# Attention and expert layers on one core: GpSimd's SBUF operations wait for VectorE's, in a new order

## The chip, the cores and the metric

The kernel runs on one core of one Trainium2 chip. The time is device microseconds of one execution; a figure for a kernel is the median of its runs. A core has five engines, each with its own queue of instructions: TensorE (PE, with its weight loads as PEld), VectorE (DVE), ScalarE (ACT), GpSimd (POOL) and SyncE (SP, which issues DMAs). GpSimd and VectorE both read and write SBUF; only VectorE of the two reads PSUM.

## The reference

Eight batches of eight heads, 576 positions, head size 64. Attention keeps only scores that lie within tau of the row's maximum; the rest go to -1e9 before the softmax. Its output, 4608 tokens of 512 values, goes through a layer of eight experts: tokens with a positive skip score go to the expert of the largest gate logit, the others pass through.

```python
scores = scale * np.matmul(q, k.transpose(0, 1, 3, 2))
thresh = np.max(scores, axis=-1, keepdims=True) - tau
scores = np.where(scores >= thresh, scores, -1000000000.0)
attn = np.exp(scores - np.max(scores, axis=-1, keepdims=True))
attn = attn / (np.sum(attn, axis=-1, keepdims=True) + 1e-09)
out = np.matmul(attn, v)
...
h = np.maximum(xc[mask] @ w1[e], 0.0)
y[mask] = gate_w[mask, None] * (h @ w2[e])
out[do_compute] = xc + y
```

## The kernel before

Work is laid out in 32 pairs of heads (`NG`, four pairs to a batch), each of nine steps. fp32 operands are split into a high and a low part, so that PE multiplies in faster types and adds the products.

For a pair, `plan_pair` (L455) loads q and k (raw), casts the high half (hl, L432 on VectorE or L430 on ScalarE) and subtracts for the low half (L487, GpSimd or VectorE, 576 columns each), and `plan_dist` and `plan_blk` let SP copy the parts to where PE reads them (QK, BD). `plan_score` (L675 to L725) computes scores once to find each row's maximum (mx, VectorE, L707), `plan_thresh` makes thresholds of them in small VectorE operations (L753 to L777), and `plan_weights` computes the scores again, transposed, with the threshold taken off (sps, L675), takes the exponential on ScalarE (e, L840), masks it on VectorE (p, L845), casts two blocks of it to fp16 (phh, 1152 columns, L430 on ScalarE or L432 on VectorE) and subtracts for the low part on GpSimd (phl, L882; tph and tpl are the same for the tail rows, 576 columns). `plan_av` multiplies with V (L909, L912, L913; L913 is the one that reads phl), and GpSimd scales the result by the reciprocal sums (xb at L958, x at L971). `plan_v` loads V of a batch (vraw), finds its largest value on VectorE (L590) and splits it (Vl, L652, GpSimd). Once per two batches, and twice at the end, `plan_gate` works out each token's expert and list slot in some twenty small VectorE operations (L1140 to L1236), and GpSimd scatters records with indirect DMAs (lst, L1264). `plan_early` (L1343 on) picks one expert early, gathers tokens for it and splits its first weights in eight pieces (L1412); `plan_sort` orders the others.

Score banks in PSUM are two of `sps` and two of `shp`: PE's next score waits until VectorE has read one. `p` has two buffers, freed by GpSimd's phl; phh and phl have three, freed by PE.

All of these steps, up to some 700 us, are first handed to a planner (`Plan`) as operations with a cost on each engine that may run them, and dependencies. `place` then goes through time: for each engine it looks at operations that could start, and puts the one with the best rank in the next slot. `port` marks an operation that uses the SBUF port which VectorE and GpSimd share: every GpSimd operation by default except indirect DMAs (`port=()`), and the VectorE operations marked `BOTH` (casts and subtractions with both operands in SBUF, gate operations). `held` keeps, for each of the two engines, when its last such operation ends, and the other engine's next such operation isn't placed before that. So in the plan these operations of the two engines never overlap. The rank comes from keys (`OFF` shifts them), and then from `SEEDS`: each seed shifts ranks of the order reached so far, by small random amounts, and plans again. The order of the last pass is the one in which the instructions are written to the engines' queues; between engines only the dependencies through data become semaphore waits.

Behind the planned stage, from some 700 us on, the other experts run in a hand-written order that doesn't pass through `Plan`.

Of the kernel before, what the change touches and what calls it, by code (L numbers as in the profile page):

```python
# [73 lines left out]
DISS = 0.65  # L74
ENGINES = ("PE", "DVE", "ACT", "POOL", "SP")
PEER = {"DVE": "POOL", "POOL": "DVE"}
SEEDS = (
    3000017, 3000028, 3000035, 3000067, 3001483, 3019621, 3115975, 3117104, 3144197,
)
DLAT = 0.9  # L80
OFF = dict(
# [3 lines left out]
class Op:  # L85
    def __init__(self, key, fn, eng, lat, off, port):
        self.key, self.fn, self.eng, self.lat, self.off, self.port = key, fn, eng, lat, off, port
        self.deps, self.succ = [], []
        self.t0 = self.t1 = self.on = self.rev = None
        self.xfer = ()  # L90

    def ready(self, e):
        r = 0.0
        for d, order in self.deps:
            x = d.t0 if order else d.t1 + d.latency(e)
            r = x if x > r else r
        return r
# [21 lines left out]


class Plan:
    def __init__(self):
        self.ops, self.rings = [], {}

    def take(self, name, bufs):
        return [(name, bufs)]
# [26 lines left out]
        o.xfer = xfer  # L153
        return o

    def place(self, links, options, ready, rank, put):
        free = dict.fromkeys(ENGINES, 0.0)
        cand = {e: [] for e in ENGINES}
        held = dict.fromkeys(PEER, 0.0)
        wait = [len(a) for a, _ in links]  # L160

        def add(i):
            for e in options(i):
                cand[e].append((ready(i, e), rank(i, e), i))

        for i, n in enumerate(wait):
            if not n:
                add(i)
        for _ in links:
            best = None  # L170
            for e in ENGINES:
                c = cand[e]
                if not c:
                    continue
                h = held[PEER[e]] if e in PEER else 0.0
                if h > free[e]:
                    c = [(h, k, i) if r < h and e in self.ops[i].port else (r, k, i) for r, k, i in c]
                m = max(free[e], min(c)[0]) + LOOK
                x = min((x for x in c if x[0] <= m), key=lambda x: (x[1], x[0]))
                t = max(free[e], x[0])  # L180
                if best is None or t < best[0]:
                    best = (t, e, x[2])
            t, e, i = best
            free[e] = put(i, e, t, free[e])
            if e in PEER and e in self.ops[i].port:
                held[e] = free[e]
            for q in options(i):
                cand[q] = [x for x in cand[q] if x[2] != i]
            for q in links[i][1]:
                wait[q] -= 1  # L190
                if not wait[q]:
                    add(q)

    def forward(self, rank, emit=False):
        link = 0.0

        def put(i, e, t, _):
            nonlocal link
            o = self.ops[i]
            o.t0, o.on = t, e  # L200
            o.t1 = end = t + o.eng[e]
            for n, x in enumerate(o.xfer):
                link = max(link, t + (n + 1) * o.eng[e] / len(o.xfer) + DISS) + x
                o.t1 = link
            if emit:
                code = o.fn.__code__
                o.fn(e) if code.co_argcount and code.co_varnames[0] == "e" else o.fn()
            return end

        self.place(self.fore, lambda i: self.opts[i], lambda i, e: self.ops[i].ready(e), rank, put)  # L210
        return max(o.t1 for o in self.ops)

    def backward(self):
        link = 0.0

        def put(i, e, t, was):
            nonlocal link
            o = self.ops[i]
            if o.xfer:
                s = max(t, link)  # L220
                link = s + sum(o.xfer)
                o.rev = s + o.length()
                return max(was, t) + o.eng[e]
            o.rev = t + o.eng[e]
            return o.rev

        ops = self.ops
        self.place(
            self.back, lambda i: (ops[i].on,), lambda i, e: ops[i].latest(), lambda i, e: -ops[i].t1, put
        )  # L230
        return [-o.rev for o in ops]

# [30 lines left out]
def attn_moe_kernel(ctx: ExitStack, tc: tile.TileContext, qk, vl, tau, wg, w1, w2, out):  # L263
    nc = tc.nc
# [137 lines left out]
    NG = B * HP  # L402
    END = STEP * NG

    pl = Plan()
    PE, DVE, ACT, POOL, SPQ = "PE", "DVE", "ACT", "POOL", "SP"
    BOTH = (DVE, POOL)

    def wtile(dt, name):
        return wraw.tile([P, WW], dt, name=name, tag="wr")  # L410
# [17 lines left out]
    def copy(e, dst, src):  # L428
        if e == ACT:
            nc.scalar.activation(dst, src, AF.Copy)  # L430
        else:
            nc.vector.tensor_copy(dst, src)  # L432
# [865 lines left out]
    class Job:  # L1298
        def __init__(self, cap, rec, ids, idg):
            self.cap, self.rec, self.ids, self.idg = cap, rec, ids, idg  # L1300
            self.nb = -(-cap // P)
# [41 lines left out]
    def plan_early(k, j):  # L1343
# [22 lines left out]
        o = T["rec0"] = pl.dma(k, l0, T["scs0"] + [(T["pick"],)], [0.1])  # L1366
# [5 lines left out]
        o = pl.op(k + 1, ids, [o], {DVE: 0.15})  # L1372
# [12 lines left out]
        hs, ls = [], []  # L1385
# [12 lines left out]
        for n in range(8):  # L1398
            i, q = divmod(n, 4)
            d, fs = n // 2, slice(n % 2 * ns, n % 2 * ns + ns)  # L1400

            def hi(e, i=i, q=q, d=d, fs=fs):
                if i == 0 and q == 0:
                    early["wh"] = ep.tile([P, nv], F32R, name="wh0", tag="vraw")
                if d == 3 and fs.start == 0:
                    early["w3"] = ep.tile([P, 2 * S], F32R, name="w3", tag="raw")
                copy(e, w_h(d, fs), early["raw"][i][:, q * ns : q * ns + ns])

            def lo(e, i=i, q=q, d=d, fs=fs):
                if q == 0:  # L1410
                    wls[i] = wtile(F32R, "wl0")[:, 0 : 2 * F]
                (nc.gpsimd if e == POOL else nc.vector).tensor_tensor(  # L1412
                    w_l(d, fs), early["raw"][i][:, q * ns : q * ns + ns], w_h(d, fs).bitcast(F32), op=ALU.subtract
                )

            deps = ring.take("vraw", 1) if n == 0 else [(hs[0],)]
            if n == 6:
                deps = deps + ring.take("raw", 1)
            hs.append(pl.op(k + 4 + n, hi, [ld1 if i else T["pick"]] + deps, {ACT: 0.52, DVE: 0.33}, port=BOTH))
            deps = [(ls[-1],)] if q else ring.take("wr", WRB)  # L1420
            ls.append(pl.op(k + 5 + n, lo, hs[-1:] + deps, {POOL: 1.225, DVE: 0.6}, port=BOTH))
            if n == 3:
                ring.free("wr", hs[0:4] + ls[0:4])
# [229 lines left out]
    ms.enter_context(tc.manual_schedule(engines={ET.PE, ET.DVE, ET.Activation, ET.Pool, ET.SP}))  # L1653
    pl.run(SEEDS)

# [373 lines left out]
```

## Time and profile before

| | us |
|---|---|
| median of 3 runs | 992.52 (987.98 to 994.86) |
| the profiled execution | 992.55 |
| its span, first to last instruction | 990.8 |
| PE busy | 889.1 (90%) |
| VectorE busy | 746.2 (75%) |
| GpSimd busy | 678.0 (68%) |
| ScalarE busy | 600.9 (61%) |
| mean granted TensorE clock | 0.962 |

Shares are means over stages with different limits, so they are read by stretch. An instruction's duration in the trace includes the time in which it has started and waits for its port. "Idle before" is time in which the engine had no instruction, and the releaser is what ended it.

### The profile page before, as it was taken

What the parts mean: (1) busy time and instruction counts of PE and PEld (TensorE: products, weight loads), DVE (VectorE), ACT (ScalarE), POOL (GpSimd) and SP (SyncE); (2) the same over time, 40 slices, a digit from 0 to 9 for tenths busy, and PEclk for the clock granted to TensorE, in tenths of its full rate; (3) what the DMA queues carried; (4) which work ended last, traced back from release to release, by engine and by line L of the source; (5) the groups of instructions that cost most, each with busy time, mean ns of one, the idle gap of its engine ahead of it and who ended that gap; (6) DMA issues with size and microseconds to landing.
All of it is one profiled execution on the core that took longest, in us unless ns stands there. A gap on an engine that the chain in (4) does not pass through costs nothing. (4 is left out here: it accounts for less than half of the span.)

```text
span 990.8 us, 24765 instructions
## 1 busy us (share of the span) xinstructions
PE 889.1 (90%) x9618; PEld 820.4 (83%) x9618; DVE 746.2 (75%) x1692; ACT 600.9 (61%) x880; POOL 678.0 (68%) x444
## 2 busy tenths in 40 slices
PE   6889999989999799899889898978869999999994
PEld 5689898888888798899878788877858998999993
DVE  6788888888888798988888998897444454567770
ACT  1567867956686596698688478657423423553440
POOL 5578987976689687689888577877633454654551
PEclk9799999999999999999999899999898999999997
DMA  7986687776449657766955954712337555535530
GB/s 200 216 195 150 141 223 173 163 225 150 102 103 250 143 128 209 202 144 149 263 112 125 275 136 88 179 20 103 113 99 247 156 179 192 180 122 182 174 127 17
DMA packets 81791, 157.37 MB, mean 159 GB/s; under 512 B 28620, under 2 KB 28876, under 8 KB 81673
## 3 DMA queue, kind: packets, MB, share of 16 engines
q1 hardware_dynamic: 76984, 145.49, 56.0%
q0 software_dynamic: 4544, 10.28, 3.2%
q8 instruction: 77, 1.26, 0.5%
q14 instruction: 42, 0.34, 0.1%
q10 hardware_dynamic: 144, 0.00, 0.0%
HBM read 70.78 MB, written 24.78 MB: 96 GB/s over the span
## 5 line engine op out<-in xcount | busy, mean ns | idle before, releaser
L882 POOL TENSOR_TENSOR phl<-p,phh 128x1152 f16<-128x1152 f32 x128 | 306.3, 2396 | 105.7 <-ACT phh L430 63.9
L840 ACT ACTIVATE e<-sps,ntau 128x576 f32<-128x576 f32 x288 | 209.1, 737 | 103.0 <-PE sps L675 92.4
L707 DVE TENSOR_REDUCE mx<-shp 128x1 f32<-128x288 f32 x558 | 238.0, 449 | 44.3 <-PE shp L702 39.5
L845 DVE SCALAR_TENSOR_TENSOR p<-sps,e 128x576 f32<-128x576 f32 x288 | 215.5, 750 | 35.1 <-ACT e L840 20.2
L702 PE MATMUL shp<-QK 128*128 128x288 f32 x992 | 207.0, 319 | 22.5 <-DVE mx L707 20.5
L675 PE MATMUL sps<-QK 128*128 128x288 f32 x1024 | 194.3, 315 | 19.5 <-DVE p L845 13.8
L702 PEld LDWEIGHTS shp<-QK 128*128 128x128 f32 x992 | 152.4, 195 | 34.3 <-DVE mx L707 29.0
L675 PEld LDWEIGHTS sps<-QK 128*128 128x128 f32 x1024 | 149.6, 194 | 30.1 <-DVE p L845 14.1
L430 ACT ACTIVATE phh<-p 128x1152 f16<-128x1152 f32 x107 | 124.2, 1161 | 32.9 <-DVE p L845 20.5
L913 PE MATMUL avp<-Vh,phl 128*128 128x65 f16 x1280 | 134.6, 196 | 8.1 <-POOL phl L882 8.0
L909 PE MATMUL avp<-Vh,phh 128*128 128x65 f16 x1280 | 136.8, 198 | 0.3 <-ACT a L430 0.3
L912 PE MATMUL avp<-Vl,phh 128*128 128x64 f16 x1280 | 135.4, 196 | 0.0
L913 PEld LDWEIGHTS <-phl 128*128 128x128 f16 x1280 | 120.3, 99 | 8.9 <-POOL phl L882 8.9
L909 PEld LDWEIGHTS <-phh 128*128 128x128 f16 x1280 | 119.0, 100 | 8.7
L912 PEld LDWEIGHTS <-phh 128*128 128x128 f16 x1280 | 120.5, 101 | 0.6 <-issue 0.4
L1682 POOL TENSOR_TENSOR wl<-wr,wh 128x1024 fp32r<-128x1024 f32 x28 | 72.5, 2605 | 34.7 <-ACT wh L1681 29.4
L1719 PE MATMUL hps<-xh,wl 128*128 128x256 f32 (+4 forms) x256 | 76.7, 300 | 0.0
L1719 PE MATMUL hps<-xh,wh 128*128 128x256 f32 (+4 forms) x248 | 76.0, 306 | 0.1
L1719 PE MATMUL hps<-xl,wh 128*128 128x256 f32 (+4 forms) x248 | 74.7, 301 | 0.0
L487 POOL TENSOR_TENSOR hl<-raw,hl 128x576 fp32r<-128x576 f32 x41 | 58.7, 1445 | 21.6 <-DVE gps L757 19.1
L1731 POOL DMA_INDIRECT out<-o,ids x21 | 21.0, 1002 | 71.6 <-DVE o L1730 30.1
L1720 ACT ACTIVATE QK<-hps 128x256 fp32r<-128x256 f32 (+4 forms) x64 | 27.0, 422 | 68.2 <-PE hps L1719 66.2
(261 smaller groups left out, 1957.4 us busy)
## 6 DMA issues: line engine op xcount, KB each, us to landing
QK<-hl SPq DMA_DIRECT2D x192, 288.0 KB
wr<-in_w SPq DMA_DIRECT2D x31, 1024.0 KB
raw<-in_qk SPq DMA_DIRECT2D x32, 576.0 KB
vraw<-in_vl SPq DMA_DIRECT2D x32, 384.0 KB
xs<-xb SPq DMA_DIRECT2D x32, 256.0 KB
out<-xb SPq DMA_DIRECT2D x32, 256.0 KB
BD<-hl SPq DMA_DIRECT2D x64, 64.0 KB
xs<-x SPq DMA_DIRECT2D x8, 128.0 KB
```

The costliest lines, as they stand in the source:

```text
L430: nc.scalar.activation(dst, src, AF.Copy)
L675: nc.tensor.matmul(ps[:, j, 0:HS], w_, x_[:, js], start=(i == 0), stop=(i == len(mm) - 1))
L702: nc.tensor.matmul(ps[:, 0:HS], w_, x_[:, js], start=(q == 0), stop=(q == len(mm) - 1))
L707: nc.vector.tensor_reduce(T["mx", g][:, o, j : j + 1], T.pop(("S", g, i, j))[:, 0:HS], AX.X, ALU.max)
L840: nc.scalar.activation(e, T["W", g, i][:, :, 0:HS], AF.Exp, bias=ntau, scale=0.125)
L845: nc.vector.scalar_tensor_tensor(T[z][:, kt % 2].rearrange("p (a b) -> p a b", a=2), T.pop(("W", g, i))[:, :, 0:HS], 0.0, T.pop(("e", g, i ...
L882: nc.gpsimd.tensor_tensor(T["pl", g, i], T.pop(z)[:, 0:nk], T["ph", g, i], op=ALU.subtract)
L909: nc.tensor.matmul(pv[:, c, :], x, Vh[:, hd, kt, :], start=(j + q + c == 0), stop=False, skip_group_check=True)
L912: nc.tensor.matmul(pv[:, c, 0:D], x, Vl[:, hd, kt, :], start=False, stop=False, skip_group_check=True)
L913: nc.tensor.matmul(pv[:, c, :], y, Vh[:, hd, kt, :], start=False, stop=(c == NM), skip_group_check=True)
L1682: lo[q % 2].tensor_tensor(w[1][:, sl], rs, w[0][:, sl].bitcast(F32), op=ALU.subtract)
L1719: nc.tensor.matmul(hp_[:, 0:cap], w_, x, start=(i == 0), stop=(i == len(mm) - 1))
```

## The change

Every operation is now written by `emit`, which notes the instructions that it makes. After a VectorE operation with `port`, the name of its last instruction is kept. The first instruction of the next GpSimd operation with `port`, in the order of the plan, gets a dependency on that name, hence a semaphore wait, and the name is cleared. Nothing is added in the other direction. In the plan, GpSimd's operation may start 0.165 us after the end of VectorE's (`LAG`; `GAL` is the mirrored figure of the backward pass). `SEEDS` is a new list, of 126 numbers in place of 9. The cast of the seventh weight piece gets an order-only dependency on the sixth's that creates its tile.

```diff
+LAG = {"DVE": 0.0, "POOL": 0.165}
+GAL = {"DVE": 0.165, "POOL": 0.0}
 SEEDS = (
-    3000017, 3000028, 3000035, 3000067, 3001483, 3019621, 3115975, 3117104, 3144197,
+    14000043, 14000049, 14000050, 14000051, 14000054, 14000501, 14000633, 14000634, 14000684, 14000705, 14000776,
...
 class Plan:
-    def __init__(self):
-        self.ops, self.rings = [], {}
+    def __init__(self, tc):
+        self.ops, self.rings, self.tc = [], {}, tc
+        self.last = None
+
+    def emit(self, o):
+        e, code, seen = o.on, o.fn.__code__, []
+        nc = self.tc.nc
+
+        def note(*a):
+            seen.append(a[-1])
+
+        nc.push_inst_callback(note)
+        o.fn(e) if code.co_argcount and code.co_varnames[0] == "e" else o.fn()
+        nc.remove_inst_callback(note)
+        if not seen:
+            return
+        if e == "DVE" and e in o.port:
+            self.last = seen[-1].name
+        elif e == "POOL" and e in o.port and self.last:
+            self.tc.add_manual_dep(
+                seen[0],
+                self.last,
+                mybir.DependencyInfo(mybir.DependencyClass.Sync, mybir.DependencyReason.DATA),
+                reason="VectorE reads SBUF first",
+            )
+            self.last = None
...
-                h = held[PEER[e]] if e in PEER else 0.0
+                h = held[PEER[e]] + lag[e] if e in PEER else 0.0
...
             if emit:
-                code = o.fn.__code__
-                o.fn(e) if code.co_argcount and code.co_varnames[0] == "e" else o.fn()
+                self.emit(o)
...
             if n == 6:
                 deps = deps + ring.take("raw", 1)
+            if n == 7:
+                deps = deps + [(hs[6],)]
```

## Rows read from the trace of the kernel before

**Rows 1.** Busy time by stretch: the stretch and its length in us, then busy us of each engine (number of instructions), the granted clock, the DMA share and GB/s.
```profile
40.00:700.00 660.00, 595.73 (x7699) 551.58 (x7699) 566.35 (x1369) 480.55 (x684) 521.91 (x303) 0.97 0.66 162
700.00:760.00 60.00, 50.69 (x444) 46.75 (x443) 22.99 (x70) 18.69 (x34) 25.96 (x22) 0.91 0.34 111
760.00:991.00 231.00, 215.97 (x1360) 199.25 (x1358) 131.07 (x187) 92.79 (x153) 113.01 (x66) 0.98 0.46 153
```

**Rows 2.** The timeline of VectorE and GpSimd from 438 to 443 us: start, duration, engine, line, operation, and in brackets the idle time before it and what ended it.
```profile
438.56 0.75 DVE L432 CAST phh<-p 128x1152 f16<-128x1152 f32 x1
...
441.13 1.05 DVE L432 CAST tph<-p 128x576 f16<-128x576 f32 x1
442.10 0.75 DVE L487 TENSOR_TENSOR hl<-raw,hl 128x576 fp32r<-128x576 f32 x1
...
439.48 2.38 POOL L882 TENSOR_TENSOR phl<-p,phh 128x1152 f16<-128x1152 f32 x1 [0.94 <-DVE phh L432]
442.26 1.74 POOL L882 TENSOR_TENSOR tpl<-p,tph 128x576 f16<-128x576 f32 x1 [0.39 <-DVE tph L432]
```

**Rows 3.** Groups of instructions by line and shape: count, busy us in all, mean ns of one, and idle time before them with its releasers.
```profile
L487 DVE TENSOR_TENSOR hl<-raw,hl 128x576 fp32r<-128x576 f32 x23 | 26.4, 1161 | 1.4 <-ACT hl L430 1.4
L432 DVE CAST phh<-p 128x1152 f16<-128x1152 f32 x21 | 16.5, 787 | 0.0
L432 DVE CAST hl<-raw 128x1152 fp32r<-128x1152 f32 x9 | 10.8, 1196 | 0.3
...
L1154 DVE TENSOR_SCALAR gw<-lg 128x9 f32<-128x9 f32 x3 | 0.5, 164 | 0.0
...
L882 POOL TENSOR_TENSOR phl<-p,phh 128x1152 f16<-128x1152 f32 x128 | 306.3, 2396 | 105.7 <-ACT phh L430 63.9 <-DVE phh L432 6.9 <-DVE ca L1164 4.6
```

**Rows 4.** The timeline of VectorE: five single instructions.
```profile
240.19 2.29 DVE L1193 TENSOR_SCALAR rec<-tokp 128x9 f32<-128x9 f32 x1
...
517.41 3.05 DVE L432 CAST hl<-raw 128x1152 fp32r<-128x1152 f32 x1
...
640.42 2.60 DVE L1173 CAST rs<-rs 128x8 bf16<-128x8 f32 x1
...
652.93 3.04 DVE L1221 TENSOR_TENSOR ca<-ca 128x32 f32<-128x32 f32 x1
...
660.79 2.56 DVE L1236 SCALAR_TENSOR_TENSOR si<-si 128x4 int32<-128x4 int32 x1
```

**Rows 5.** The timeline of GpSimd at the same places; x2 merges two instructions with no pause between them.
```profile
240.08 2.38 POOL L882 TENSOR_TENSOR phl<-p,phh 128x1152 f16<-128x1152 f32 x1
...
515.10 4.74 POOL L882 TENSOR_TENSOR phl<-p,phh 128x1152 f16<-128x1152 f32 x2
...
640.61 2.37 POOL L882 TENSOR_TENSOR phl<-p,phh 128x1152 f16<-128x1152 f32 x1
...
653.61 1.30 POOL L882 TENSOR_TENSOR tpl<-p,tph 128x576 f16<-128x576 f32 x1
654.85 1.06 POOL L958 TENSOR_TENSOR xb<-a,z 128x512 f32<-128x512 f32 x1
...
660.93 2.39 POOL L882 TENSOR_TENSOR phl<-p,phh 128x1152 f16<-128x1152 f32 x1
```

**Rows 6.** The timeline of VectorE and of GpSimd at 693 us.
```profile
692.98 5.17 DVE L1412 TENSOR_TENSOR wl<-raw,wh 128x512 fp32r<-128x512 f32 x1
...
692.90 4.70 POOL L882 TENSOR_TENSOR phl<-p,phh 128x1152 f16<-128x1152 f32 x2
```

**Rows 7.** The timeline of PE: the first instruction after each of nine gaps, with the gap in brackets.
```profile
243.17 0.85 PE L702 MATMUL shp<-QK 128*128 128x288 f32 x2 [1.89 <-DVE mx L707]
...
262.48 0.80 PE L675 MATMUL sps<-QK 128*128 128x288 f32 x4 [2.14 <-DVE p L845]
...
415.22 0.90 PE L702 MATMUL shp<-QK 128*128 128x288 f32 x4 [1.92 <-DVE mx L707]
...
520.96 0.53 PE L702 MATMUL shp<-QK 128*128 128x288 f32 x2 [2.88 <-DVE mx L707]
...
560.79 0.17 PE L1205 MATMUL gps<-rs,tri 128*128 128x8 bf16 x1 [2.54 <-DVE rs L1173]
...
614.34 0.77 PE L675 MATMUL sps<-QK 128*128 128x288 f32 x4 [2.03 <-DVE p L845]
...
643.08 0.17 PE L1205 MATMUL gps<-rs,tri 128*128 128x8 bf16 x1 [1.75 <-DVE rs L1173]
...
656.62 0.54 PE L702 MATMUL shp<-QK 128*128 128x288 f32 x2 [2.02 <-DVE mx L707]
...
664.40 0.80 PE L675 MATMUL sps<-QK 128*128 128x288 f32 x4 [2.85 <-DVE p L845]
```

**Rows 8.** Busy time by stretch, columns as in rows 1: one of five stretches with a low granted clock (243.13 to 246.54, 263.61 to 267.02, 560.57 to 567.40, 615.19 to 618.60, 666.39 to 673.22), and the sum of the five.
```profile
560.57:567.40 6.83, 6.37 (x49) 5.97 (x49) 5.71 (x16) 1.79 (x2) 3.52 (x3) 0.50 0.80 207
...
sum 23.89, PE 23.38 PEld 22.07 DVE 16.13 ACT 8.20 POOL 14.28; mean PE 4.68 PEld 4.42 DVE 3.23 ACT 1.64 POOL 2.85
```

**Rows 9.** Waits by who waited for whom over the whole span: us in total, times, and the longest in us.
```profile
DVE vmx L590 <- DMA vraw<-in_vl: 11.7, 8, 2.1
DVE p L845 <- POOL phl L882: 10.8, 7, 5.0
...
PE avp L913 <- POOL phl L882: 8.0, 6, 4.8
```

**Rows 10.** The timeline of GpSimd at 327 us.
```profile
327.69 0.40 POOL L971 TENSOR_TENSOR x<-a,z 64x128 f32<-64x128 f32 x1 [4.26 <-DMA lst<-rec,si]
```

More of the change, by code (lines that the diff above doesn't have):

```diff
@@ L154, in dma, with place @@
         return o
-    def place(self, links, options, ready, rank, put):
+    def place(self, links, options, ready, rank, put, lag):
         free = dict.fromkeys(ENGINES, 0.0)
@@ L205, in put @@
             if emit:
-                code = o.fn.__code__
-                o.fn(e) if code.co_argcount and code.co_varnames[0] == "e" else o.fn()
+                self.emit(o)
             return end
-        self.place(self.fore, lambda i: self.opts[i], lambda i, e: self.ops[i].ready(e), rank, put)
+        self.place(self.fore, lambda i: self.opts[i], lambda i, e: self.ops[i].ready(e), rank, put, LAG)
         return max(o.t1 for o in self.ops)
@@ L228, in backward @@
         self.place(
-            self.back, lambda i: (ops[i].on,), lambda i, e: ops[i].latest(), lambda i, e: -ops[i].t1, put
+            self.back, lambda i: (ops[i].on,), lambda i, e: ops[i].latest(), lambda i, e: -ops[i].t1, put, GAL
         )
@@ L403, in attn_moe_kernel @@
     END = STEP * NG
-    pl = Plan()
+    pl = Plan(tc)
     PE, DVE, ACT, POOL, SPQ = "PE", "DVE", "ACT", "POOL", "SP"
```

11 rows, old and new, of the table SEEDS are left out of this document.

## The prediction

> **What bounds the kernel now.** I read the page's busy shares first, then busy time by stretch. From 40 to 700 us (attention) PE works 595.73 of 660 us, VectorE (DVE) 566.35, GpSimd (POOL) 521.91; from 760 on the two vector engines have ample room [rows 1]. So PE is the bound of the attention stage, with 64.3 us of idle time in it, and VectorE is close behind. The change touches only the planned stage, so a gain has to come out of those 64.3 us, or out of TensorE's clock there.
>
> Next I asked which groups on VectorE are longer than their work. An SBUF subtraction of 576 columns takes 0.75 us when nothing disturbs it, at 442.10 [rows 2], but the mean of 23 is 1161 ns; the casts hl<-raw average 1196 ns where the equally wide phh<-p average 787; the small gate operations need about 0.16 us [rows 3]. GpSimd's long instruction, phl<-p, takes 2.4 us [rows 3]. Then I looked for single VectorE instructions that were far too long. Nine of them end a PE gap; five are shown [rows 4]: a cast of 128x8 takes 2.60 us, a 128x32 subtraction 3.04. Each time a GpSimd SBUF instruction starts close to VectorE's, before it (240.08 against 240.19) or even after it (640.61 against 640.42, 660.93 against 660.79), and is served first [rows 5]; at 517.41 the cast ends only with the second of two phl, at 652.93 the subtraction only with an xb that follows a tpl. The clearest pair stands at 693: one subtraction is held for 5.17 us by two phl that follow each other without a pause [rows 6]. So a VectorE instruction that is waiting does not get in when GpSimd's current instruction ends, if GpSimd has another one ready: it loses each of those races. The plan gives the two engines the SBUF port in turn, but nothing on the chip keeps that turn.
>
> Behind VectorE's held instruction stand the row maxima (mx) and masks (p) that free the score banks, and PE stops for them. The nine gaps are 1.89, 2.14, 1.92, 2.88, 2.54, 2.03, 1.75, 2.02 and 2.85 us, **20.0 us** together [rows 7], almost a third of PE's idle time of the stage. After five of them the granted clock is 0.50, the 1.2 GHz level, for 3.41 or 6.83 us: 23.89 us in all, with PE busy for 23.38 of it [rows 8]. At the upper level that work takes half, so these stretches cost up to **11.7 us**.
>
> **The change part by part.**
>
> *The wait.* A GpSimd SBUF instruction now starts after the VectorE SBUF instruction planned ahead of it. All nine cases look like a turn that was planned for VectorE and lost: VectorE's queue held ready mx and p behind the instruction, and a plan that gave GpSimd the first turn would have put those ahead. One of nine I leave out as doubtful. Of a gap, part is won back today, since the other engines catch up during it; the stage is idle for 44.3 of 660 us outside the nine, 6.7%, so PE has something, but not much, to win back from. I count two thirds as real, for gap and clock alike: (20.0 + 11.7) x 8/9 x 2/3 = **18.8 us gained**. The bounds are 0 (all of it comes back as other idle time) and 31.7 us.
>
> *What the wait costs.* Where VectorE is first today, GpSimd's instruction is issued and held by the port: the tpl at 442.26 takes 1.74 us, against 1.30 for one with the port to itself, and ends at 444.00 [rows 2, 5]. With the wait it would start 0.08 to 0.17 us after VectorE's end (those are the lags from tph, 441.13 + 1.05, to the tpl and from phh, 438.56 + 0.75, to the phl [rows 2]): 442.85 + 0.08 to 0.17 + 1.30 is 444.23 to 444.32, so 0.2 to 0.3 us more. I take at most 100 handovers (53 VectorE instructions of rows 3 and some ten in each of five runs of gate operations; the latter count is an estimate): 100 x 0.3 = 30 us of GpSimd's time at most, little over nothing at the least, where GpSimd is not ready yet anyway. GpSimd is idle for 138 us of the stage [rows 1], which covers it. Behind a waiting phl stand the next phl, the head's output scaling (xb, x) and the indirect DMAs of GpSimd's queue; PE's last matmuls of a head (L913) and, through the two p buffers, VectorE's own masks wait for phl. These waits are 8.0 us of PE's and 10.8 of VectorE's today [rows 9]. If GpSimd's lateness grows by 15 us, the middle of the bounds, and a fifth reaches PE: **3 us lost**, between 0 and 15.
>
> *The lag in the planner's costs* (0.165 us) adds no work; it is inside that price. *The order-only dependency of the seventh weight cast on the sixth* costs nothing: the two pieces come from one load, and their casts follow each other anyway; without that cover it is the wait for one cast of 512 columns, less than the 787 ns of a phh, which is over twice as wide [rows 3].
>
> *The new order.* All five queues are ordered afresh, SP's loads and GpSimd's indirect DMAs with them, while the count of instructions and bytes stays. I cannot see the new order in this trace. What it can shift is bounded by gaps unconnected with the port: VectorE waits 11.7 us for V loads, and the phl waits just named [rows 9]; together some 20 us with PE's share below that. I take no change, and 10 us either way for the range.
>
> The sum: -18.8 + 3 = -15.8. The profiled execution took 992.55 us (span 990.8 and 1.7 around it), and the median of the three runs is 992.52, so the same base serves. **Forecast 977 us.** The stage behind it is a chain of PE work that starts when attention ends, so the gain is carried to the end whole.
>
> **The port's rule.** By the Trainium skill (SBUF — State Buffer, section Who interferes with whom) the pair is locked for a whole instruction, and issue order decides who is blocked. By that, the VectorE instruction at 693 would have got in after the first phl, at 2.3 us; the trace has it in after the second, and so disagrees [rows 6].
>
> **The rivals.**
>
> *Served in order of arrival.* If the port does serve by arrival, and the four cases with GpSimd's last instruction starting after VectorE's own (517.41, 640.42, 652.93, 660.79) had another cause, their gaps of 2.88 + 1.75 + 2.02 + 2.85 = 9.5 us stay. By the same fractions the gain is then 10.5/20.0 of 18.8 = 9.9 less 3: 985.6 us. This is what the skill's rule above would make of it. Rows 6 speak against it. Chance 0.08.
>
> *The new order brings its own gaps.* The new order may meet V loads and phl at worse moments. With the 10 us of the bound lost, 977 becomes 987 to 990. For it: PE has 44 us of such gaps already. Against: nothing in the trace says that the present order is lucky. Chance 0.20.
>
> *Slower: GpSimd becomes the late one.* The wait hangs GpSimd on VectorE's queue, which itself waits for PE and ScalarE. The trace shows the price of a late GpSimd once: it stood for 4.26 us [rows 10], and the longest waits of rows 9 lie behind that, VectorE's mask with 5.0 us and PE with 4.8. If a VectorE instruction runs behind its planned time by one phl (2.4 us) at ten of the handovers and all of that reaches PE, 24 us are lost, with some clock (3.41 us at half, three times, 5 us): 977 + 29 = 1006 us. It decides once more than about six such waits reach PE whole. Against: 138 us idle on GpSimd, and three phh/phl buffers. Chance 0.14.
>
> *The change does nothing that PE sees,* because the held instructions were planned after GpSimd's: then the wait isn't on those pairs, and the time is 992 give or take the order. Against: the starts so close to each other, and the ready work behind. Chance 0.06.
>
> **How the numbers follow.** The forecast case has 0.52, with 966 to 984 as its own range. About 1%, 982.6 to 1002.4, is what a measurement of this kernel can tell from no change. Faster: nearly all of the forecast case (0.48), some of the order's case and of the arrival case (0.07), 0.55. Slower: the late GpSimd, 0.14. The rest, 0.31, is within 1%. The range starts at 962, the forecast with nearly the whole bound won, and goes up to 1000, past the order's own gaps; the slower rival stays outside.
>
> **What would show it.** The 2 to 5 us VectorE instructions on tiny gate operands are gone from the attention stage, and the mean of the subtraction (1161 ns) falls to below 0.9 us; rows of GpSimd carry idle time ended by VectorE's casts, subtractions and gate operations; PE's idle time from 40 to 700 falls from 64 to some 50 us and the clock's mean rises. The forecast is wrong if the held instructions vanish and PE's idle time stays: then waits for phl, or for loads, have grown by as much. It is also wrong if they remain.

## The result: 965 us, and the profile after

The changed kernel takes 965.21 us (median of 4 runs, 956.40 to 969.93) against 993.69 for the kernel before, measured beside it (median of 4, 987.98 to 996.08): ratio 0.9711 [0.9626, 0.9797], 28.5 us less. The forecast was 977 with a range from 962 to 1000: the direction and the main mechanism hold, the gain is larger than predicted. The profiled execution is the fastest of the four, 956.40 us with a span of 954.6, so its differences to before (36.2 us by the spans) are some 8 us larger than those of the medians.

Where did the time go? First the busy time by stretch, columns as in [rows 1], cut where the planned work ends: the first matmul of the experts' second layer, at 726.30 us before and 692.40 after. Before:

```profile
40.00:726.30 686.30, 620.49 (x7986) 576.01 (x7985) 577.34 (x1410) 492.25 (x704) 533.98 (x313) 0.97 0.64 160
726.30:990.80 264.50, 241.90 (x1512) 221.56 (x1512) 143.08 (x216) 99.78 (x167) 126.89 (x78) 0.97 0.44 149
```

After, where the last line is the stretch of [rows 1]:

```profile
40.00:692.40 652.40, 607.88 (x7994) 565.30 (x7992) 551.89 (x1424) 500.01 (x713) 513.56 (x302) 0.99 0.68 169
692.40:954.60 262.20, 243.28 (x1512) 223.24 (x1512) 142.08 (x208) 99.72 (x167) 125.69 (x78) 0.96 0.44 150
40.00:700.00 660.00, 615.49 (x8019) 571.37 (x8018) 556.45 (x1427) 502.75 (x715) 519.17 (x306) 0.99 0.67 167
```

The planned stage is 33.9 us shorter (686.30 to 652.40), the rest of the kernel as long as before within 2.3 us. In the stage PE does the same number of matmuls (7986 and 7994). Its idle time, stretch less busy time, falls from 65.8 to 44.5 us: 21.3. Its busy time falls by 12.6 us, and the stage's granted clock rises from 0.97 to 0.99; busy time times clock is 602 us in both, so the clock accounts for the shorter busy time. So the gain has the two parts that the prediction named, gaps and clock.

Next the groups on VectorE. Of before, the two small operations of which [rows 4] shows single cases (2.29 and 2.60 us):

```profile
L1173 DVE CAST rs<-rs 128x8 bf16<-128x8 f32 x5 | 5.5, 1095 | 0.2
...
L1193 DVE TENSOR_SCALAR rec<-tokp 128x9 f32<-128x9 f32 x3 | 4.7, 1578 | 0.0
```

After, where lines of the code stand 36 further down (L487 is L523, L1193 is L1229):

```profile
L523 DVE TENSOR_TENSOR hl<-raw,hl 128x576 fp32r<-128x576 f32 x34 | 29.2, 877 | 0.2 <-ACT hl L466 0.2
L468 DVE CAST hl<-raw 128x1152 fp32r<-128x1152 f32 x8 | 6.7, 843 | 0.5 <-DMA raw<-in_qk 0.4
L1209 DVE CAST rs<-rs 128x8 bf16<-128x8 f32 x5 | 1.2, 248 | 0.2
L1229 DVE TENSOR_SCALAR rec<-tokp 128x9 f32<-128x9 f32 x3 | 0.5, 181 | 0.0
```

The subtraction's mean is 877 ns where it was 1161, the cast's 843 where it was 1196, rs 248 where it was 1095, and rec 181 where it was 1578 (the first two means of before stand in [rows 3]). The longest hold that is left is a cast near the end of the stage, at 656.75: 1.98 us for two columns. Before, twelve VectorE instructions of the stage (from 40 us on) took 2 us or more; now none does.

How a turn is kept now, in the timeline of ScalarE and VectorE at 384 us:

```profile
383.25 1.16 ACT L466 ACTIVATE phh<-p 128x1152 f16<-128x1152 f32 x1 [2.47 <-DVE p L881]
...
384.40 0.16 DVE L1245 TENSOR_TENSOR co<-cnt,eoff 128x8 f32<-128x8 f32 x1
```

and of GpSimd at the same place:

```profile
384.73 2.39 POOL L918 TENSOR_TENSOR phl<-p,phh 128x1152 f16<-128x1152 f32 x1 [3.90 <-DVE co L1245]
```

GpSimd has been idle for 3.90 us, but mostly for its operand: phh ends at 384.41. co ends at 384.56, and the phl starts 0.17 us later, so the wait for co itself costs about 0.15 us. VectorE's co takes its 0.16 us, and PE does not wait for this phl. The waits by who waited for whom (columns as in [rows 9]):

```profile
DVE p L881 <- POOL phl L918: 8.8, 13, 2.6
...
PE avp L949 <- POOL phl L918: 7.1, 9, 3.6
POOL tpl L918 <- DVE hl L523: 6.9, 6, 1.7
POOL phl L918 <- DVE co L1245: 5.1, 2, 3.9
```

The last two are handovers that end GpSimd's idle time: hl and co are no operands of tpl and phl. A row names what came last, not what the wait cost: of co's longest wait, 3.9 us, all but 0.15 are for phh, and [rows 3] has a ca in such a place before, without any handover. The waits for a late phl have not grown: PE's are 7.1 us where they were 8.0, VectorE's masks' 8.8 where they were 10.8 [rows 9].

In the planned stage three stretches with a low granted clock are left (from 385.39, 484.37 and 655.04 us), 13.65 us long. Before there were nine, 40.95 us long: the five of [rows 8], 23.89 us, and four more, from 150.97, 219.24, 331.88 and 697.11 us, that the prediction did not tie to held instructions. Half of the 27.3 us between the two sums is 13.7, close to the 12.6 us by which PE's busy time fell. The sum of the three:

```profile
sum 13.65, PE 12.75 PEld 11.78 DVE 9.30 ACT 5.52 POOL 11.17; mean PE 4.25 PEld 3.92 DVE 3.10 ACT 1.84 POOL 3.72
```

The longest of them, 6.83 us from 484.37 on, comes with the longest PE gap that is left from 40 us on in the planned stage, in the timeline of PE:

```profile
485.18 0.23 PE L949 MATMUL avp<-Vh,phl 128*128 128x65 f16 x1 [3.60 <-POOL phl L918]
```

### The profile page after: what moved, and what is told of

Same layout as the page of the kernel before. It is cut to its first block, busy times and chain, and to the rows that moved or that the text cites. A ratio compares the mean times of both kernels' runs of the same rounds, so it can differ in the third digit from the quotient of the medians.

```text
span 954.6 us, 24785 instructions
## 1 busy us (share of the span) xinstructions
PE 877.5 (92%) x9618; PEld 810.4 (85%) x9618; DVE 720.3 (75%) x1697; ACT 607.0 (64%) x887; POOL 655.6 (69%) x432
## 5 line engine op out<-in xcount | busy, mean ns | idle before, releaser
L876 ACT ACTIVATE e<-sps,ntau 128x576 f32<-128x576 f32 x288 | 208.8, 735 | 60.8 <-PE sps L711 55.6
L881 DVE SCALAR_TENSOR_TENSOR p<-sps,e 128x576 f32<-128x576 f32 x288 | 216.0, 752 | 30.2 <-ACT e L876 18.3
L711 PE MATMUL sps<-QK 128*128 128x288 f32 x1024 | 191.0, 311 | 15.8 <-DVE p L881 13.6
L711 PEld LDWEIGHTS sps<-QK 128*128 128x128 f32 x1024 | 146.2, 190 | 26.8 <-DVE p L881 13.1
L466 ACT ACTIVATE phh<-p 128x1152 f16<-128x1152 f32 x113 | 131.1, 1160 | 35.5 <-DVE p L881 26.9
L949 PE MATMUL avp<-Vh,phl 128*128 128x65 f16 x1280 | 131.0, 195 | 7.3 <-POOL phl L918 7.1
L945 PE MATMUL avp<-Vh,phh 128*128 128x65 f16 x1280 | 133.4, 196 | 1.9 <-ACT a L466 1.9
L948 PE MATMUL avp<-Vl,phh 128*128 128x64 f16 x1280 | 132.2, 194 | 0.0
L949 PEld LDWEIGHTS <-phl 128*128 128x128 f16 x1280 | 118.0, 98 | 8.7 <-POOL phl L918 8.4
L945 PEld LDWEIGHTS <-phh 128*128 128x128 f16 x1280 | 117.1, 98 | 8.5
L948 PEld LDWEIGHTS <-phh 128*128 128x128 f16 x1280 | 118.3, 99 | 2.2 <-issue 2.1
L1719 ACT ACTIVATE wh<-wr 128x1024 fp32r<-128x1024 f32 x60 | 60.6, 1051 | 1.2 <-DMA out<-xb 1.2
```

The source lines that it names most:

```text
L711: nc.tensor.matmul(ps[:, j, 0:HS], w_, x_[:, js], start=(i == 0), stop=(i == len(mm) - 1))
L876: nc.scalar.activation(e, T["W", g, i][:, :, 0:HS], AF.Exp, bias=ntau, scale=0.125)
L881: nc.vector.scalar_tensor_tensor(T[z][:, kt % 2].rearrange("p (a b) -> p a b", a=2), T.pop(("W", g, i))[:, :, 0:HS], 0.0, T.pop(("e", g, i ...
L945: nc.tensor.matmul(pv[:, c, :], x, Vh[:, hd, kt, :], start=(j + q + c == 0), stop=False, skip_group_check=True)
L948: nc.tensor.matmul(pv[:, c, 0:D], x, Vl[:, hd, kt, :], start=False, stop=False, skip_group_check=True)
L949: nc.tensor.matmul(pv[:, c, :], y, Vh[:, hd, kt, :], start=False, stop=(c == NM), skip_group_check=True)
```

## The experiments

Times are medians; "before" is the kernel before, measured beside the run. Ratios carry a 95% interval. The last two columns are of the profiled execution, from 40 us to the end of the planned stage as above: PE's idle time, and how many VectorE instructions took 2 us or more. The kernel before has 65.8 us and 12 there, the changed kernel 44.5 and 0.

| run | order | GpSimd waits for | us | before | ratio | PE idle | 2 us and more |
|---|---|---|---|---|---|---|---|
| e1 | old | planned port operations | 965.81 | 991.34 | 0.9716 [0.9658, 0.9774] | 49.8 | 3 |
| e2 | new | none | 973.01 | 991.34 | 0.9809 [0.9743, 0.9874] | 55.8 | 5 |
| e3 | third | planned port operations | 966.71 | 991.34 | 0.9731 [0.9675, 0.9786] | 52.1 | 2 |
| e4 | third | none | 989.88 | 991.34 | 0.9979 [0.9949, 1.0009] | 61.8 | 10 |
| e6 | old | gate operations only | 964.72 | 988.95 | 0.9729 [0.9683, 0.9774] | 49.0 | 3 |
| e7 | old | casts and subtractions only | 980.35 | 988.95 | 0.9872 [0.9809, 0.9935] | 54.3 | 10 |
| e8 | new | any VectorE operation | 986.06 | 988.95 | 0.9959 [0.9933, 0.9984] | 64.3 | 4 |
| e10 | new | gate operations only | 969.78 | 993.01 | 0.9763 [0.9700, 0.9826] | 52.1 | 3 |
| e11 | new | planned port operations (the changed kernel) | 962.50 | 993.01 | 0.9719 [0.9648, 0.9790] | 45.6 | 0 |
| e12 | old | port operations, only behind an indirect DMA | 985.25 | 991.40 | 0.9939 [0.9903, 0.9974] | 60.8 | 9 |

**The wait apart from the order (e1, e2).** e1 has the order of before and the wait of the change:

```diff
-LAG = {"DVE": 0.0, "POOL": 0.165}
-GAL = {"DVE": 0.165, "POOL": 0.0}
 SEEDS = (
-    14000043, 14000049, 14000050, 14000051, 14000054, 14000501, 14000633, 14000634, 14000684, 14000705, 14000776,
...
+    3000017, 3000028, 3000035, 3000067, 3001483, 3019621, 3115975, 3117104, 3144197,
...
-                h = held[PEER[e]] + lag[e] if e in PEER else 0.0
+                h = held[PEER[e]] if e in PEER else 0.0
...
-            if n == 7:
-                deps = deps + [(hs[6],)]
```

> The order of the kernel before, unchanged, with the wait alone. If the wait makes the gain (theory of the forecast), the nine held VectorE instructions of the kernel before are gone or below 1 us and the time falls by 15 to 25 us, to 968 to 978 us. If the gain is the new order's (rival), the time stays within 985 to 1000 us. If a late GpSimd is a real price, this order, which was planned without the lag, shows it: PE's and VectorE's waits for phl exceed the 8.0 and 10.8 us of before, and the time is over 1000.

Measured: 25.5 us less than before, as much as the whole change within the intervals. In the very order of before the nine held instructions that end PE gaps are gone: matched one by one, they take 0.15 to 0.76 us, and the nine gaps of [rows 7] are gone with them. Not every hold is: the subtraction still has a mean of 1035 ns. e1's groups (L1196 is the rs cast, L1216 rec, L510 the subtraction), then in the timeline of VectorE two of the nine, the instructions that were at 517.41 and 652.93 [rows 4]:

```profile
L510 DVE TENSOR_TENSOR hl<-raw,hl 128x576 fp32r<-128x576 f32 x23 | 23.5, 1035 | 1.2 <-ACT hl L453 1.2
L1196 DVE CAST rs<-rs 128x8 bf16<-128x8 f32 x5 | 0.9, 172 | 0.2
L1216 DVE TENSOR_SCALAR rec<-tokp 128x9 f32<-128x9 f32 x3 | 0.5, 157 | 0.0
...
511.87 0.76 DVE L455 CAST hl<-raw 128x1152 fp32r<-128x1152 f32 x1
...
634.09 0.19 DVE L1244 TENSOR_TENSOR ca<-ca 128x32 f32<-128x32 f32 x1
```

and the planned stage by e1's windows:

```profile
40.00:703.80 663.80, 614.00 (x7994) 570.94 (x7992) 554.99 (x1412) 493.17 (x706) 528.27 (x313) 0.98 0.66 166
```

PE idles 49.8 us (663.80 - 614.00), 16.0 less than before, and is busy 6.5 less. One gap grew, in e1's timelines of GpSimd and PE at 323 us:

```profile
323.86 0.40 POOL L994 TENSOR_TENSOR x<-a,z 64x128 f32<-64x128 f32 x1 [6.61 <-DMA lst<-rec,si]
...
328.08 0.24 PE L936 MATMUL avp<-Vh,phl 128*128 128x65 f16 x1 [7.16 <-POOL phl L905]
```

This is the stand of [rows 10], 4.26 us before: GpSimd's x ends its idle time late, and the phl behind it is what PE waits for, 7.16 us where it was 4.80 (at 331.91). In both runs the landing of an indirect DMA ends the stand, and VectorE has no port operation from 317.88 to 328 us in e1, so nothing here shows that the longer gap is a price of the wait.

e2 is the changed kernel without the wait (LAG in the plan stays):

```diff
         if e == "DVE" and e in o.port:
             self.last = seen[-1].name
-        elif e == "POOL" and e in o.port and self.last:
-            self.tc.add_manual_dep(
...
-            self.last = None
```

> The new order without the semaphore wait (everything else as in the changed kernel). If the wait makes the gain, VectorE instructions held for 2 us and more are back in the attention stage, PE's gaps behind them too, and the time is 980 to 995 us. If the gain is the new order's, it stays at 960 to 972.

Measured: 18.3 us less than before. So the new order alone is worth a good part of the gain too, and the wait adds only 8 to 10 us to it. The time, 973.01 us, lies between the two ranges. Held instructions are back, as expected if the wait makes the gain, but fewer of them: five of 2 us and more where the kernel before has twelve. The rs casts (221 ns) and rec (160) are clear of GpSimd in this order; four other gate operations and the subtraction are not. e2's group of the subtraction, then three of the gate operations in the timeline of VectorE (the fourth is a gw at 385.01, 2.20 us):

```profile
L515 DVE TENSOR_TENSOR hl<-raw,hl 128x576 fp32r<-128x576 f32 x34 | 36.7, 1098 | 2.1 <-ACT hl L458 2.1
...
624.69 3.05 DVE L1182 TENSOR_SCALAR gw<-lg 128x4 f32<-128x4 f32 x1
...
632.29 2.29 DVE L1189 TENSOR_TENSOR ca<-ioem,gw 128x32 f32<-128x32 f32 x1
...
637.28 2.35 DVE L1205 TENSOR_TENSOR_SCAN ca<-seg,ca 128x32 f32<-128x32 f32 x1
```

PE gaps of 2.29 us (at 628.15) and 2.18 us (at 640.43) stand behind the first and the last of them.

**A third order, with and without the wait (e3, e4).** The search is stopped after the first 60 of the new seeds, which gives another order; e4 leaves the wait out as e2 does.

```diff
 SEEDS = (
     14000043, 14000049, 14000050, 14000051, 14000054, 14000501, 14000633, 14000634, 14000684, 14000705, 14000776,
...
-    14041956, 14048043, 14052847, 14055232, 14061885, 14063003, 14066037, 14071628, 14072296, 14074187, 14074771,
...
 )
```

> A third order: only the first 60 of the 126 seeds, with the wait. It shows what an order is worth by itself. If orders with the wait are worth about the same, 965 to 978 us; if the last 66 seeds carry the gain, 980 and more.

> The third order without the wait. If the wait's worth doesn't depend on the order, this is 15 to 25 us slower than the third order with it; if it was special to one order, the two are within 8 us of each other.

Measured: 966.71 with the wait and 989.88 without, 23.2 us apart. Without the wait, three orders from the same planner take 991, 973 and 990 us; with it, 965.8, 965.2 and 966.7. With the wait it hardly matters which of these plans it is. Without it the time goes with the number of held instructions: 12, 5 and 10 of 2 us and more. It does so roughly in the whole table, but for e8, where GpSimd is late. That the orders differ for this reason is argued, not shown.

**Which operations carry the gain (e6, e7, e10, e11).** On the old order the wait is set only after VectorE operations that no other engine may run (gate, pick and sort, e6), or only after the casts and subtractions that could have gone elsewhere (e7). e10 is the cut of e6 on the new order, and e11 the changed kernel again, measured beside e10.

```diff
-        if e == "DVE" and e in o.port:
+        if e == "DVE" and e in o.port and len(o.eng) == 1:
             self.last = seen[-1].name
```

e7 has `len(o.eng) > 1` there.

> The order of the kernel before; GpSimd waits only for VectorE's gate, pick and sort operations (those that only VectorE can run). Seven of the nine gaps of the kernel before stood behind such operations: 1.89 + 2.14 + 1.92 + 2.54 + 1.75 + 2.02 + 2.85 = 15.1 of 20.0 us. If gaps are worth their length with their clock, three quarters of the 25.5 us of the wait in this order: 968 to 976 us. If the many larger casts and subtractions are what counts, 980 to 990.

> The order of the kernel before; GpSimd waits only for VectorE's casts and subtractions of 512 columns and more. By the gaps, a quarter of the gain (2.88 + 2.03 = 4.9 us of 20.0): 982 to 988 us. If the larger ones count, 966 to 975.

> The new order; GpSimd waits for VectorE's gate, pick and sort operations alone. In the old order that was as good as the full wait (964.7 against 965.8 us). If the waits for large operations are worth nothing in the new order too, 958 to 967 us; if they are needed there, where 34 subtractions of 576 columns are VectorE's in place of 23, 967 to 973.

> The changed kernel once more, beside the one above: 956 to 970 us as in its first four runs.

Measured: 24.2 us from the small operations alone (e6), below the times expected of it, and 8.6 from the large ones (e7), a little better than expected. In e7 the small ones are as long as before:

```profile
L1196 DVE CAST rs<-rs 128x8 bf16<-128x8 f32 x5 | 5.5, 1096 | 0.2
L1216 DVE TENSOR_SCALAR rec<-tokp 128x9 f32<-128x9 f32 x3 | 4.8, 1593 | 0.0
```

The two gains sum to more than e1's 25.5 by their medians, so they overlap: a wait for a gate operation also keeps GpSimd behind the subtractions that VectorE has run before it (in e6 the subtraction that was held at 609.97 takes 0.75 us, though no wait is set for it). In the new order, where VectorE has 34 subtractions in place of 23, waiting for the gate alone leaves 7.3 us on the table by the medians (969.78 against 962.50; the two intervals overlap). Two groups are longer in e10 than in e11: the subtraction, with a mean of 1086 ns against 886 (6.8 us in all), and four weight pieces, 2494 against 677 ns (7.3 us in all). The weight pieces in e10, and PE's gaps behind the two that are held longest (at 665.05 and 677.51, by phl that follow indirect DMAs):

```profile
L1448 DVE TENSOR_TENSOR wl<-wr,wh 128x512 fp32r<-128x512 f32 x4 | 9.9, 2494 | 0.0
...
668.62 2.29 PE L711 MATMUL sps<-QK 128*128 128x288 f32 x8 [3.66 <-DVE p L881]
...
683.62 1.33 PE L711 MATMUL sps<-QK 128*128 128x288 f32 x4 [2.23 <-DVE p L881]
```

and the pieces in e11:

```profile
L1448 DVE TENSOR_TENSOR wl<-wr,wh 128x512 fp32r<-128x512 f32 x4 | 2.6, 677 | 0.0
```

So there the waits for large operations are needed too; how much of the difference is the subtraction's and how much the weight pieces', no run tells.

**The price of a late GpSimd (e8).** GpSimd waits for the last VectorE operation of any kind planned ahead, maxima and masks included, which have no turn on the port in the plan (masks take 750 ns in the mean before and 752 after):

```diff
-        if e == "DVE" and e in o.port:
+        if e == "DVE":
             self.last = seen[-1].name
```

> The new order; GpSimd's SBUF operations wait for the last VectorE operation of any kind planned ahead of them, masks and maxima too, which take no turn on the port. It puts a price on hanging GpSimd on VectorE's queue. If a late GpSimd is what costs (the slower rival), PE's waits for phl grow from some 7 to over 20 us and the time rises by 10 us or more, to 975 to 1000. If GpSimd's idle time covers it, 962 to 970.

Measured: 986.06 us; nearly all of the gain is gone. The waits show how:

```profile
POOL phl L918 <- DVE p L881: 27.0, 16, 4.3
...
DVE p L881 <- POOL phl L918: 25.0, 34, 2.7
...
PE avp L949 <- POOL phl L918: 19.5, 32, 2.7
```

GpSimd waits 27.0 us for masks, VectorE's next masks wait 25.0 us for phl to free their buffers, and PE's wait for phl goes from 7.1 us in 9 cases to 19.5 in 32. Its idle time in the stage is 64.3 us, 19.8 above the changed kernel's. Its busy time, 619.83 us, is 12 us above as well, at a granted clock of 0.99 in both; what this is stays open. The slower rival's mechanism exists, then; the change stays clear of it by waiting for the port's users alone.

**How the port is given (e5, e9, e12).** Two small kernels measure it; both leave attention and experts out and write zeros. e5 lets GpSimd run one, two or three subtractions of 1152 columns in a row, and starts a VectorE operation just after the first of them:

```python
nc.vector.tensor_reduce(m, buf[:, 0:S], AX.X, ALU.max)
for i in range(n):
    nc.gpsimd.tensor_tensor(ds_[i], buf[:, S:], b, op=ALU.subtract)
if small:
    nc.vector.tensor_copy(c16, x2[:, 0:E])
else:
    nc.vector.tensor_tensor(c, x2, y, op=ALU.subtract)
```

> The port by itself: attention and the experts are left out, so the output is zeros. In each round VectorE first reduces 576 columns (about 0.65 us) while GpSimd starts one, two or three subtractions of 1152 columns (2.4 us each) in a row; then VectorE issues an SBUF subtraction of 576 columns (0.75 us free of holds), in later rounds a cast of 128x8 (about 0.16). If the port is given in order of arrival, VectorE's instruction lasts the same 2.5 us (1.9 for the cast) behind one, two or three. If GpSimd's next instruction goes ahead of a waiting VectorE, it lasts about 2.5, 4.9 and 7.3 us (1.9, 4.3 and 6.7 for the cast).

The timeline of e5, one case with the VectorE subtraction and one with the small cast, three GpSimd subtractions in both:

```profile
75.53 7.51 POOL L82 TENSOR_TENSOR d<-buf,b 128x1152 f16<-128x1152 f32 x3 [0.62 <-ACT buf L79]
76.09 2.42 DVE L86 TENSOR_TENSOR c<-x,y 128x576 f32<-128x576 f32 x1
...
158.62 7.00 POOL L82 TENSOR_TENSOR d<-buf,b 128x1152 f16<-128x1152 f32 x3 [0.61 <-ACT buf L79]
159.18 1.83 DVE L84 CAST c<-x 128x8 bf16<-128x8 f32 x1
```

VectorE's subtraction ends at 78.51. GpSimd's first needs 2.36 us, to 77.89, so VectorE got in behind it, with two more queued; it is GpSimd's second that waits (7.51 us for three in place of 7.00). The cast ends at 161.01, with the first one. The means over all 15, whatever the number of GpSimd subtractions, are 2403 and 1838 ns. Here the port is given in order of arrival, and "it loses each of those races" is false.

e9 puts an indirect DMA ahead of GpSimd's subtractions, and either a chain of 14 small casts on VectorE that begins ahead of the DMA, or one cast that begins just after the first subtraction:

```python
nc.gpsimd.indirect_dma_start(
    g,
    None,
    xs[:, :],
    bass.IndirectOffsetOnAxis(ap=idx, axis=0),
...
)
for i in range(n):
    nc.gpsimd.tensor_tensor(ds_[i], buf[:, S:], b, op=ALU.subtract)
if chain:
    nc.vector.tensor_reduce(m[:, 0:1], buf[:, S - 8 : S], AX.X, ALU.max)
    for i in range(CASTS):
        nc.vector.tensor_copy(c16[:, i], x2[:, 0:E])
```

> The port behind an indirect DMA; attention and the experts are left out, so the output is zeros. GpSimd issues an indirect DMA of 128 rows and then one, two or three subtractions of 1152 columns that wait for nothing. VectorE issues 14 casts of 128x8 in a row meanwhile; in later rounds one cast some 0.4 us into the first subtraction. If GpSimd's next SBUF instruction claims the port while the indirect DMA is still on (theory), the first casts take 0.15 us, and one that starts 0.3 us or more after the DMA's start, before the first subtraction's own start, lasts until the end of that subtraction (2.4 us and more). If GpSimd then keeps the port from instruction to instruction, that cast lasts 3, 5.4 and 7.8 us with one, two and three subtractions, and the late cast 2, 4.4 and 6.8 us. If the port goes by order of arrival here too, as it did without the indirect DMA (2.4 us, however many), the casts before the first subtraction all take 0.15 us and the late cast 2 us in all three.

The timeline of e9: chains with one, two and three subtractions (x14 merges the casts), then the late cast with three:

```profile
71.12 4.05 DVE L100 CAST c<-x 128x8 bf16<-128x8 f32 x14
71.28 1.02 POOL L87 DMA_INDIRECT g<-xs,idx  x1 [1.53 <-ACT buf L86]
72.33 2.37 POOL L96 TENSOR_TENSOR d<-buf,b 128x1152 f16<-128x1152 f32 x1
...
83.28 6.37 DVE L100 CAST c<-x 128x8 bf16<-128x8 f32 x14
...
84.49 4.68 POOL L96 TENSOR_TENSOR d<-buf,b 128x1152 f16<-128x1152 f32 x2
...
105.01 8.68 DVE L100 CAST c<-x 128x8 bf16<-128x8 f32 x14
...
190.08 6.99 POOL L96 TENSOR_TENSOR d<-buf,b 128x1152 f16<-128x1152 f32 x3
190.13 6.99 DVE L104 CAST c<-x 128x8 bf16<-128x8 f32 x1
```

The chain takes 4.05, 6.37 and 8.68 us: 2.3 more with each further subtraction. It ends 0.47 us (five casts) behind the last of GpSimd's subtractions each time (71.12 + 4.05 = 75.17, against 72.33 + 2.37 = 74.70). Taken singly in the trace, the cast that starts 0.41 us into the DMA is held for 3.05 us, and the one ahead of it, at 0.33 us, takes its 0.16 (in two of the other chains one at 0.34 us is held already). So behind an indirect DMA GpSimd has the port from a third of a microsecond into the DMA on, well ahead of its own subtraction's start, and keeps it from one subtraction to the next. The late cast, 0.05 us behind the first subtraction's start, also gets in only after the third: 6.99 us. It came earlier than e5's VectorE operations, which mostly began 0.56 us behind that start, so whether GpSimd keeps the port to the end because of the DMA or because VectorE asks so early is not parted by these runs. That the port is taken before the subtraction starts is shown by the chain, and it is the instruction behind that takes it, not the DMA itself: in the trace of before, where another DMA follows the one that begins at 657.39, VectorE's si at 657.88 and pk at 657.95 take 0.15 and 0.16 us.

This is what [rows 4] to [rows 6] showed at five places. In GpSimd's timeline of before, an indirect DMA stands directly ahead of the phl and tpl in each of them:

```profile
514.08 1.00 POOL L1264 DMA_INDIRECT lst<-rec,si  x1 [0.17 <-PE shp L702]
...
639.57 1.01 POOL L1264 DMA_INDIRECT lst<-rec,si  x1 [0.56 <-PE sps L675]
...
652.60 1.00 POOL L1264 DMA_INDIRECT lst<-rec,si  x1 [0.15 <-issue]
...
659.94 0.97 POOL L1264 DMA_INDIRECT lst<-rec,si  x1 [0.30 <-issue]
...
691.34 1.53 POOL L419 DMA_INDIRECT xg<-xs,id  x1 [0.31 <-issue]
```

e12 asks what these alone are worth: on the old order, only a GpSimd port operation directly behind an indirect DMA waits.

```diff
         if e == "DVE" and e in o.port:
             self.last = seen[-1].name
-        elif e == "POOL" and e in o.port and self.last:
+        elif e == "POOL" and e not in o.port:
+            self.behind = True
+        elif e == "POOL" and not self.behind:
+            self.last = None
+        elif e == "POOL" and self.last:
             self.tc.add_manual_dep(
...
             self.last = None
+        if e == "POOL" and e in o.port:
+            self.behind = False
```

> The order of the kernel before; only a GpSimd SBUF operation that directly follows an indirect DMA in GpSimd's queue waits for VectorE. Three of the nine gaps stood at such places (640.61, 653.61 and 660.93: 1.75 + 2.02 + 2.85 = 6.6 of 20.0 us). If held instructions behind indirect DMAs and near ties are worth the same by their gaps, this has a third of the 25.5 us of the wait: 980 to 987 us. If the instructions that are passed by several of GpSimd's make the gain, 966 to 975; if the near ties do, 987 to 994.

Measured: 6.2 us less than before, as expected. rec stays held, rs in part:

```profile
L1222 DVE TENSOR_SCALAR rec<-tokp 128x9 f32<-128x9 f32 x3 | 4.7, 1581 | 0.0
L1202 DVE CAST rs<-rs 128x8 bf16<-128x8 f32 x5 | 3.0, 609 | 0.2
```

Of the nine held instructions three are cured, those at 640.42, 652.93 and 660.79, and six are not. So a quarter of e1's 25.5 us comes from the waits directly behind a DMA. The rest needs the others. The cast of 517.41 is among them (3.02 us in e12): GpSimd's first phl stands behind a DMA, and the cast is passed by the second. In the other five no DMA stands directly ahead, and there, by e5, a turn is lost when GpSimd's instruction arrives a little ahead of the VectorE operation that was planned first. 0.1 us is enough, as at 240.08 against 240.19 [rows 4, 5].

## Why the prediction was right, and where it was off

**What bounds the kernel.** Right. PE's idle time from 40 to 700 us falls from 64.3 to 44.5 us (660.00 - 615.49) (the forecast said some 50), and the clock of the stage rises.

**The wait's gain.** The mechanism is shown by e1, in the order of before. The mis-sized term is "I count two thirds as real, for gap and clock alike", 18.8 us with the doubtful ninth left out. e1 gives 25.5 by its medians, and none of the nine was doubtful: all nine are gone there, with their gaps. In e1's profile PE's idle time fell by 16.0 us, against 20.0 x 8/9 x 2/3 = 11.9 counted, and that is net of the gap at 328 us that grew by 2.4; so little of a gap was being won back. PE's busy time fell by 6.5, against 11.7 x 8/9 x 2/3 = 6.9. But that profile is of the slowest of e1's four executions (970.54 us, mean clock 0.962; the others have 0.965 to 0.969). By the medians 25.5 - 16.0 = 9.5 us are left for the clock (an estimate), so its share was counted too small as well, if by less. Holds that end no gap hardly come into it: matched one by one, VectorE's port operations are 24.3 us shorter in e1 than before, and 21.4 of that is in the nine.

**The wait's cost, 3 us of 0 to 15.** Not to be seen: PE waits 7.1 us for phl after the change and 9.2 in e1, 8.0 before, and the one wait that grew in e1, by 2.4 us, is ended by a DMA. The bound was a real one: e8 pays it, and more.

**The new order, 0 with 10 either way.** Right in the sum, for the wrong reason. With the wait, three orders lie within 1.5 us. Without it the new one is worth 18 us, outside the bound. It loses fewer turns (five instructions of 2 us and more in e2, twelve before), which is the likely cause and not shown by itself. "I take no change" holds only beside the wait; the two gains are largely the same one.

**"It loses each of those races."** Wrong as a statement about the port. e5 has order of arrival, one instruction at a time; only behind an indirect DMA does GpSimd have the port early and keep it (e9). The prediction generalised from five places that all stand behind such a DMA. By the Trainium skill (SBUF — State Buffer, section Who interferes with whom) whoever issues first has the pair for the whole instruction: e5 agrees (some 2.4 us with one, two or three GpSimd instructions queued), e9 disagrees (6.99 us with three). The forecast didn't hang on which it is, since a GpSimd instruction that has not been issued cannot win by either. The traces bear this out behind a DMA too: in e2 the gw at 624.69, 0.39 us into an indirect DMA, is held for 3.05 us by the phl behind; in the changed kernel, where the phl waits for VectorE first, the same gw, as far into its DMA at 612.81, takes 0.15, and the phl starts as close behind the DMA as in e2.

**The rivals.** *Order of arrival* had the port right for plain neighbours, but its consequence, 9.5 us of gaps that stay, fell: the wait cured those four places as well. *The new order's own gaps* did not come. *The late GpSimd* is a real price (e8, some 24 us), not reached here. *Nothing changes* fell with e1.

**What would show it.** The subtraction's mean fell below 0.9 us in the changed kernel (877 ns), though not in e1 (1035), which has nearly the same time: a sign of the mechanism, no measure of the gain. No gate operation is held for 2 us any more, and VectorE's hl and co end GpSimd's idle time, as foretold, though a row of that kind alone proves little (a ca stands in one before, [rows 3]).

Open: why GpSimd has the port early behind an indirect DMA, and why the new order loses fewer turns without the wait (LAG in its plan may do it, or chance; the third order has LAG too and loses ten). Waits in the hand-written stage behind, where GpSimd's wl subtractions follow gathers, were not tried; in the changed kernel two small VectorE operations are still held there for 8.01 us (cm, at 850.41) and 7.13 us (ej, at 881.23). No run beats the changed kernel; e1, e3 and e6 equal it within their intervals.

## What to carry to other kernels

Where two engines share a port, look for instructions that take several times the duration of their like, and ask whose turn it was: a planned turn that nothing enforces is lost by 0.1 us, and a lost turn of a small operation on the critical path costs a whole long one. A semaphore from the engine whose work PE waits for to the one that has room is cheap (0.17 us of lag here), as long as it waits only for operations that use the port (e8 lost nearly all of the gain by waiting for others). Test the handover and the order apart, since a lucky order can hide more than half of what the handover is worth.

## What was not expected of the hardware

- Behind an indirect DMA, GpSimd's next instructions hold the shared port from about a third of a microsecond into the DMA, 0.6 us ahead of the first one's start, until the last of those that follow each other without a pause: a cast of eight columns (0.16 us) took 3.05 us with one subtraction behind the DMA, and the chain around it 2.3 us more with each further one.
- Without the DMA the same neighbours alternate in order of arrival, and a GpSimd instruction waits for VectorE as VectorE does for it (7.51 us for three in place of 7.00).
- Small operations decide: waiting for the gate operations alone, most of them of 0.16 to 0.3 us, gave 24.2 us in the order of before, where the full wait gave 25.5.
